# MLP token blocks of 384 and 512 columns, and weight tiles walked there and back

## The chip, the cores and the metric

The kernel runs on one core of a Trainium2 chip. The metric is the device time of that core in microseconds. TensorE does the matmuls, VectorE (DVE), ScalarE (ACT) and GpSimd (POOL) the work between them, and SyncE (SP) issues the DMAs.

## The reference

```python
def _attn_ref(q, k, v):                      # (4, 12, 448, 64) each
    scores = scale * np.matmul(q, k.transpose(0, 1, 3, 2))
    scores = np.where(mask, -1000000000.0, scores)      # causal
...
    return np.matmul(attn, v).astype(np.float32)
def _moe_ref(x, w1, w2, w3, w_out):          # x (1792, 768), d_ff 1024
    a = x @ w1
    b = x @ w2
    h = a * b @ w3
    return (h @ w_out).astype(np.float32)
def _moe2_ref(x, w_in, w_out):               # d_ff 2048
    h = x @ w_in
    g = h - np.tanh(h)
    return (g @ w_out).astype(np.float32)
def reference(**kwargs):
...
    x = np.ascontiguousarray(attn_out.transpose(0, 2, 1, 3)).reshape(B * S, H * D)
    x = _moe_ref(x=x, **moe_kwargs)
    return _moe2_ref(x=x, **moe2_kwargs)
```

## The kernel before

Activations lie transposed: features on the partitions, tokens along the columns. The 1792 tokens are taken in two halves of W = 896 columns, and each half of the MLPs in two blocks of S = 448 columns, one batch each. Every MLP operand is kept as a high and a low part (fp32r, `[P, 2, ...]`), and a product of one weight tile of 128 x 128 with one block is three matmuls in a row into one PSUM buffer, high by low, low by high, high by high (lines 406 to 408, in `gemms`). A product over 6, 8 or 4 such tiles is thus 18, 24 or 12 matmuls; each matmul has a weight load of its own.

The stages of a half, in order:
- `bilinear`: for each of 8 groups of 128 columns of W1 and W2, a weight tile `hl` of W1 (s = 0) and then one of W2 (s = 1), each with both blocks, 18 matmuls a block. Behind a product of W1, `keep` copies it to `asb`; behind one of W2, `mult` multiplies by `asb` (line 788), and `split` writes the high part (line 262) and the low part (line 265) of the result into the tile `g`.
- `project`: 6 weight tiles of W3·W_out, each with both blocks, 24 matmuls a block, reading `g`, writing `x` (the second half's is `x2`). That product of weights is made at the start of the kernel, beside attention, by matmuls of 384 columns (`product`).
- `Second.up`: 16 weight tiles of w_in, in four quarters q of 4, 18 matmuls a block. `finish` computes h - tanh(h) from the PSUM buffer, with tanh for large h and a polynomial for small, in some 12 instructions on ACT and DVE and a `split` into `g`, whose low part GpSimd writes.
- `Second.down`: for each quarter 6 weight tiles `w` of w_out, 12 matmuls a block, added up in `acc`; in the last quarter each block goes out by DMA (line 915).

The up products of a quarter and the down products of the quarter before are mixed by `paced`. While the second half goes through `bilinear` and `project`, the weights w_in and w_out are converted from float64 on DVE, ACT and POOL (tiles `raw`, `t`, `cvo`).

The order of the instructions on every engine comes from a planner (`Plan`): each strand of work is a generator that asks for a tile of a ring, an event or an engine with an assumed cost, such as `act(n)`, `dve(n)` or `pe(n, 3)`, and at each step the strand that could start first goes next. A ring hands out its buffers in turn. PSUM holds two buffers `mm`, to which six more, `mm2`, come once attention is over; these serve `project` of the second half and all that follows (`rings`).

Of the kernel before, what the change touches and what calls it, by code (L numbers as in the profile page):

```python
# [19 lines left out]
F32 = mybir.dt.float32  # L20
# [7 lines left out]
P = 128  # L28
# [3 lines left out]
NP = H // 2  # L32
W = 2 * S
OFF = [0, 112, 336, 672, 1120]

# [195 lines left out]
def body(ctx: ExitStack, tc: tile.TileContext, qkd, vd, vd4, w12, w3t, wo, w_in, wo2, out):  # L231
# [161 lines left out]
    def gemms(ring, n, products):  # L393
# [5 lines left out]
        for k in range(last + 1):  # L399
            for buf, (w, x, needs, finish) in zip(bufs, products):  # L400
# [366 lines left out]

    def bilinear(tiles, batches, x, xr, r_asb, ab, ab_ready):

        for j in range(8):  # L770
            asb, have = [None, None], [Event(), Event()]
            for s in range(2):
                wt = tiles[2 * j + s]
                yield wt.ready
                for t in batches:
                    tk = slice(t * S, (t + 1) * S)

                    def keep(buf, t=t, asb=asb, have=have):
                        asb[t] = yield r_asb
                        copy((yield [act(S, True), dve(S)]), asb[t].t[:, :S], buf.t[:, :S])  # L780
                        plan.done(buf)
                        plan.set(have[t])

                    def mult(buf, t=t, asb=asb, have=have, j=j, tk=tk):
                        yield have[t]
                        yield dve(S)
                        a = asb[t].t[:, :S]
                        V.tensor_tensor(out=a, in0=buf.t[:, :S], in1=a, op=ALU.mult)  # L788
                        plan.done(buf)
                        o = ab[j // 4].t  # L790
                        yield from split(S, o[:, 0, j % 4, tk], o[:, 1, j % 4, tk], a)
                        plan.done(asb[t])
                        plan.set(ab_ready[t][j])

                    def w(k, wt=wt):
                        return cols(wt.buf.t, k)

                    def xk(k, tk=tk):
                        return x[:, 0, k, tk], x[:, 1, k, tk]
                    yield from gemm(r_mm, S, w, xk, [[xr[t][k]] for k in range(NP)], (keep, mult)[s])  # L800
                plan.done(wt.buf)

    def project(tiles, ab, ab_ready, y, y_ready, rings):

        for m in range(6):
            wt = tiles[m]
            yield wt.ready
            for t in range(2):
                tk = slice(t * S, (t + 1) * S)

                def finish(buf, t=t, tk=tk, m=m):
                    hi, lo = y[:, 0, m, tk], y[:, 1, m, tk]
                    yield act(S, True)
                    A.copy(out=hi, in_=buf.t[:, :S])
                    yield dve(S)
                    sub("DVE", lo, buf.t[:, :S], hi.bitcast(F32))
# [9 lines left out]
                yield from gemm(next(rings), S, w, xk, [[ab_ready[t][k]] for k in range(8)], finish)  # L826
            plan.done(wt.buf)
        for a in ab:
            plan.done(a)


    class Second:
# [6 lines left out]

        def up(self, q, i):  # L840

            if i == 0:
                self.g[q] = yield r_g
                self.g_ready[q] = grid(2, 4)
            mm, t = divmod(i, 2)
            m = 4 * q + mm
            tk = slice(t * S, (t + 1) * S)
            wt = self.w_up[m]
            r = self.gp

            def finish(buf):
                h = buf.t[:, :S]
                sq, g = (yield r["sq"]), (yield r["g"])
                yield act(S, True)
                A.activation(out=sq.t, in_=h, func=AF.Square)  # L855
                th = yield r["th"]
                yield act(S, True)
                A.activation(out=th.t, in_=h, func=AF.Tanh)  # L858
                yield dve(S)
                V.scalar_tensor_tensor(out=g.t, in0=sq.t, scalar=LEAD, in1=h, op0=ALU.mult, op1=ALU.mult)  # L860
                yield dve(S)
                V.tensor_tensor(out=th.t, in0=h, in1=th.t, op=ALU.subtract)
                plan.done(buf)
                for k in range(3):
                    rk = yield r["r"]
                    yield act(S + 130)
                    A.activation(out=rk.t, in_=sq.t, func=AF.Square, bias=cst[:, k:k + 1])  # L867
                    if k == 2:
                        mk = yield r["r"]
                        if (yield [act(S + 130), dve2(S)]) == "ACT":  # L870
                            A.activation(out=mk.t, in_=sq.t, func=AF.Relu, bias=cst[:, 3:4])
                        else:
                            V.tensor_scalar(out=mk.t, in0=sq.t, scalar1=1.0, scalar2=None, op0=ALU.is_gt)
                        plan.done(sq)
                    yield dves(S)
                    V.scalar_tensor_tensor(out=g.t, in0=rk.t, scalar=QUAD[k][1], in1=g.t, op0=ALU.add, op1=ALU.mult)  # L876
                    plan.done(rk)
                yield dves(S)
                V.copy_predicated(out=g.t, mask=mk.t.bitcast(U32), data=th.t)
                plan.done(mk)  # L880
                plan.done(th)
                o = self.g[q].t
                yield from split(S, o[:, 0, mm, tk], o[:, 1, mm, tk], g.t)
                plan.done(g)
# [8 lines left out]
            yield from gemm(next(self.rings), S, w, xk, [[self.y_ready[t][k]] for k in range(NP)], finish,  # L893
                            [wt.buf] if t == 1 else [])

        def down(self, q, i):

            if self.acc is None:
                self.acc = yield self.acc_ring
            m, t = divmod(i, 2)  # L900
            tk = slice(t * S, (t + 1) * S)
            wt = self.w_down[6 * q + m]

            def finish(buf):
                a = self.acc.t[:, m, tk]
                if q == 0:
                    copy((yield [act(S, True), dve(S)]), a, buf.t[:, :S])
                else:
                    yield dve(S)
                    V.tensor_tensor(out=a, in0=buf.t[:, :S], in1=a, op=ALU.add)  # L910
                plan.done(buf)
                if q == 3:
                    yield dma(P * S * 4)
                    o = self.half * W + t * S
                    SP.dma_start(out=out[m, :, o:o + S], in_=a)
                    self.left -= 1
# [10 lines left out]
            yield from gemm(next(self.rings), S, w, xk, [[self.g_ready[q][t][k]] for k in range(4)], finish,  # L927
                            ([wt.buf] if t == 1 else []) + ([self.g[q]] if i == 11 else []))

# [24 lines left out]
    def first_half(cv, r_raw, r_t, x):  # L954
# [3 lines left out]
        for _ in range(2):  # L958
            ab.append((yield r_g))
        yield from bilinear(jobs_12, (0, 1), x.t, x_ready[:2], r_asb, ab, ab_ready[0])  # L960
        plan.done(x)
# [28 lines left out]
    with tc.tile_pool(name="late", bufs=1) as late, tc.tile_pool(name="mm2", bufs=1, space=PSUM) as mm2:  # L990
# [15 lines left out]
        def second_half(cv):  # L1006
            x = yield r_x2
            plan.spawn(fetch_x(x.t), -1)
            r_asb = Ring(cv, [P, S], F32, "asb", 4)
# [4 lines left out]
            yield from bilinear(w12s, (0, 1), x.t, x_ready[2:], r_asb, ab, ab_ready[1])  # L1014
            plan.done(x)
# [10 lines left out]
        with tc.tile_pool(name="gp", bufs=1) as gp:  # L1026
            rg = {k: Ring(gp, [P, S], F32, k, n) for k, n in (("sq", 2), ("th", 2), ("g", 3), ("r", 3))}
            r_acc = Ring(gp, [P, NP, W], F32, "acc", 1)
# [3 lines left out]
            def last():  # L1032
# [59 lines left out]
```

## Time and profile before

| | us |
|---|---|
| three timed runs | 1081.27, 1087.62, 1089.7 |
| their median | 1087.62 |
| the profiled execution | 1082.89 |
| its span, first to last instruction | 1081.1 |
| TensorE with a matmul in flight | 1054.2 |

The profile is one execution. Attention and the making of the weight products fill its first part, with the first half's `bilinear` from 183 to 366 us beside attention; then `project` to 424, the second half's `bilinear` to 542 and `project` to 600, and up and down products to 1077. Matmul records overlap, since a matmul's record runs to its last output, while the next one has begun: how fast TensorE goes is read from starts, not from the lengths of records.

### The profile page before, as it was taken

The page shows a single profiled execution, that of the slowest core. Times are in us where ns is not written, and L with a number is a line of the kernel's source. Part 1 is how long each engine was busy: PE and PEld are TensorE (multiplying, and loading weights), DVE is VectorE, ACT ScalarE, POOL GpSimd, SP SyncE. Part 2 cuts the span into 40 slices and gives each one's busy share as a digit, 9 for nine tenths or more (in the row PEclk, how much of TensorE's full clock was granted, in tenths as well). Part 3 has the DMA queues.
Part 4 walks back from the last instruction along what each step waited for, and adds up shares of the span by engine and source line. Part 5 has one row for each costly group of instructions (what it writes and reads, how often), then busy time and mean ns, then how long its engine had stood idle before and what let it go on. Part 6 is the DMA issues. An engine that isn't in the chain of part 4 may idle for free.

```text
span 1081.1 us, 19824 instructions
## 1 busy us (share of the span) xinstructions
PE 1054.2 (98%) x7680; PEld 927.5 (86%) x7680; DVE 643.9 (60%) x1319; ACT 617.3 (57%) x1354; POOL 230.0 (21%) x184
## 2 busy tenths in 40 slices
PE   6799999999999999999999999999999999999998
PEld 3577788788888999899999998999999999999997
DVE  7875556577563266565556576474756655374742
ACT  6998868787784244343333578563636456553620
POOL 3532132122223100123432222121111111110210
PEclk8999999999999999999999999999999999999999
DMA  7674359787652699999999632323333543233124
GB/s 260 208 215 162 112 169 305 254 284 250 235 190 107 221 340 313 314 337 336 323 346 321 257 117 88 117 98 107 108 109 113 176 142 99 93 113 117 40 90 149
DMA packets 72317, 209.03 MB, mean 193 GB/s; under 512 B 6112, under 2 KB 23008, under 8 KB 70688
## 3 DMA queue, kind: packets, MB, share of 16 engines
q1 hardware_dynamic: 72224, 207.77, 56.8%
q8 instruction: 60, 0.98, 0.4%
q14 instruction: 33, 0.27, 0.1%
HBM read 155.45 MB, written 52.30 MB: 192 GB/s over the span
## 4 chain that ended last, share of the span: by engine, by line
PE 79%; DMA 7%; DVE 7%; ACT 4%; issue 2%; POOL 1%; SPq 0%; DVEq 0%; ACTq 0%; POOLq 0%
PE mm L406 24%; PE mm L408 23%; PE mm L407 23%; DMA raw<-wo 4%; PE pv L671 3%; PE sc L645 2%; DVE t L312 1%; DVE p L447 1%; DVE t L309 1%; DVE t L316 1%; DMA raw<-w_in 1%; PE att L529 1%; DMA sco<-cvo 1%; PE att L476 1%; ACT p L489 1%
## 5 line engine op out<-in xcount | busy, mean ns | idle before, releaser
L406 PE MATMUL mm<-x,hl 128*128 128x448 f32 x768 | 286.4, 373 | 0.4 <-DVE asb L788 0.4
L407 PE MATMUL mm<-x,hl 128*128 128x448 f32 x768 | 282.0, 367 | 0.0
L408 PE MATMUL mm<-x,hl 128*128 128x448 f32 x768 | 282.0, 367 | 0.0
L406 PEld LDWEIGHTS mm<-x,hl 128*128 128x128 f32 x768 | 144.6, 188 | 17.9 <-issue 2.3
L408 PEld LDWEIGHTS mm<-x,hl 128*128 128x128 f32 x768 | 144.6, 188 | 13.1
L407 PEld LDWEIGHTS mm<-x,hl 128*128 128x128 f32 x768 | 144.7, 188 | 12.2
L265 POOL TENSOR_TENSOR g<-g 128x448 fp32r<-128x448 f32 x64 | 75.1, 1174 | 363.0 <-ACT g L262 363.0
L876 DVE SCALAR_TENSOR_TENSOR g<-r,g 128x448 f32<-128x448 f32 x192 | 124.4, 660 | 32.8 <-ACT r L867 29.5
L406 PE MATMUL mm<-g,w 128*128 128x448 f32 x384 | 141.4, 368 | 1.2 <-POOL g L265 1.2
L408 PE MATMUL mm<-g,w 128*128 128x448 f32 x384 | 141.3, 368 | 0.0
L407 PE MATMUL mm<-g,w 128*128 128x448 f32 x384 | 141.3, 368 | 0.0
L867 ACT ACTIVATE r<-sq,cst 128x448 f32<-128x448 f32 x192 | 121.8, 665 | 8.5 <-DVE g L876 8.4
L406 PE MATMUL mm<-g,hl 128*128 128x448 f32 (+1 forms) x320 | 116.9, 365 | 2.0 <-POOL g L265 2.0
L408 PE MATMUL mm<-g,hl 128*128 128x448 f32 (+1 forms) x320 | 113.5, 355 | 0.0
L407 PE MATMUL mm<-g,hl 128*128 128x448 f32 (+1 forms) x320 | 113.4, 354 | 0.0
L860 DVE SCALAR_TENSOR_TENSOR g<-sq,mm 128x448 f32<-128x448 f32 x64 | 39.7, 621 | 102.1 <-ACT th L858 102.1
L299 ACT ACTIVATE raw<-raw 128x512 uint32<-128x512 uint32 (+1 forms) x80 | 64.0, 800 | 54.3 <-DMA raw<-wo 23.6
L309 DVE TENSOR_SCALAR t<-raw 128x512 uint32<-128x512 uint32 (+1 forms) x80 | 51.6, 645 | 71.1 <-DMA raw<-wo 34.2
L855 ACT ACTIVATE sq<-mm 128x448 f32<-128x448 f32 x64 | 34.8, 543 | 102.8 <-PE mm L408 95.4
L265 POOL TENSOR_TENSOR hl<-t,hl 128x512 fp32r<-128x512 f32 (+1 forms) x32 | 52.2, 1636 | 147.6 <-ACT hl L262 112.5
L910 DVE TENSOR_TENSOR acc<-mm,acc 128x448 f32<-128x448 f32 x72 | 44.8, 622 | 62.5 <-PE mm L408 62.5
L406 PEld LDWEIGHTS mm<-g,w 128*128 128x128 f32 x384 | 72.1, 188 | 8.9 <-POOL g L265 1.6
(78 smaller groups left out, 1616.5 us busy)
## 6 DMA issues: line engine op xcount, KB each, us to landing
hl<-sci SPq DMA_DIRECT2D x32, 768.0 KB, 4.7
w<-sco SPq DMA_DIRECT2D x48, 512.0 KB, 3.5
raw<-w SPq DMA_DIRECT2D x16, 768.0 KB, 6.3
sc<-hl SPq DMA_DIRECT2D x16, 768.0 KB, 5.8
hl<-scp SPq DMA_DIRECT2D x12, 1024.0 KB, 7.3
raw<-w_in SPq DMA_DIRECT2D x16, 768.0 KB, 7.4
sci<-cvo SPq DMA_DIRECT2D x16, 768.0 KB, 6.9
hl<-sc SPq DMA_DIRECT2D x16, 768.0 KB, 5.8
```

The costliest lines, as they stand in the source:

```text
L265: (V if eng == "DVE" else G).tensor_tensor(out=out, in0=in0, in1=in1, op=ALU.subtract)
L299: A.activation(out=u, in_=u, func=AF.Copy, scale=2.0 ** -29)
L309: V.tensor_scalar(out=t, in0=raw[:, :n, 1], scalar1=3, scalar2=0x3FFFFFF8, op0=ALU.logical_shift_left, op1=ALU.bitwise_and)
L406: PE.matmul(ps, wh, xl, start=k == 0, stop=False)
L407: PE.matmul(ps, wl, xh, start=False, stop=False)
L408: PE.matmul(ps, wh, xh, start=False, stop=k == last)
L671: PE.matmul(ps.t[e * D:(e + 1) * D, a, have[0] * 32:P], v.t[r, kb, e], x, start=kb == 0, stop=kb == block(a, 4 - 1))
L855: A.activation(out=sq.t, in_=h, func=AF.Square)
L860: V.scalar_tensor_tensor(out=g.t, in0=sq.t, scalar=LEAD, in1=h, op0=ALU.mult, op1=ALU.mult)
L867: A.activation(out=rk.t, in_=sq.t, func=AF.Square, bias=cst[:, k:k + 1])
L876: V.scalar_tensor_tensor(out=g.t, in0=rk.t, scalar=QUAD[k][1], in1=g.t, op0=ALU.add, op1=ALU.mult)
L910: V.tensor_tensor(out=a, in0=buf.t[:, :S], in1=a, op=ALU.add)
```

## The change

The two blocks of a half become columns 0 to 383 and 384 to 895 (`BLOCKS`). The second reads tokens of both batches, so it waits for the inputs of both. Every size in `bilinear`, `project`, `up` and `down` follows the block, and the rings `asb`, `sq`, `th`, `g` and `r` of these stages get tiles of 512 columns. `there_and_back` gives the order of the blocks: 0, 1 for one weight tile, 1, 0 for the next, through all stages. `up` and `down` come to `paced` by weight tiles (4 and 6 a quarter, two blocks each) and no longer by blocks (8 and 12).

```diff
+BLOCKS = [(0, 384, (0,)), (384, 512, (0, 1))]
+BIG = 512
...
+    turn_at = [0]
+
+    def there_and_back():
+
+        turn_at[0] ^= 1
+        return (0, 1) if turn_at[0] else (1, 0)
+
...
                 wt = tiles[2 * j + s]
                 yield wt.ready
-                for t in batches:
-                    tk = slice(t * S, (t + 1) * S)
-
-                    def keep(buf, t=t, asb=asb, have=have):
+                for t in there_and_back():
+                    o, n, batches = BLOCKS[t]
+                    tk = slice(o, o + n)
+
+                    def keep(buf, t=t, n=n, asb=asb, have=have):
                         asb[t] = yield r_asb
-                        copy((yield [act(S, True), dve(S)]), asb[t].t[:, :S], buf.t[:, :S])
+                        copy((yield [act(n, True), dve(n)]), asb[t].t[:, :n], buf.t[:, :n])
...
-                    yield from gemm(r_mm, S, w, xk, [[xr[t][k]] for k in range(NP)], (keep, mult)[s])
+                    yield from gemm(r_mm, n, w, xk, [[xr[b][k] for b in batches] for k in range(NP)], (keep, mult)[s])
...
-            for t in range(2):
-                tk = slice(t * S, (t + 1) * S)
-
-                def finish(buf, t=t, tk=tk, m=m):
+            for t in there_and_back():
+                o, n, _ = BLOCKS[t]
+                tk = slice(o, o + n)
+
+                def finish(buf, t=t, n=n, tk=tk, m=m):
...
-        def up(self, q, i):
-
-            if i == 0:
+        def tile(self, kind, q, i):
+
+            for n, t in enumerate(there_and_back()):
+                yield from (self.up, self.down)[kind](q, i, t, n == 1)
+
+        def up(self, q, mm, t, last):
+
+            if q not in self.g:
...
-                        parts[0] += ([lambda z=z, q=q, i=i: z.up(q, i) for i in range(8)])
+                        parts[0] += ([lambda z=z, q=q, i=i: z.tile(0, q, i) for i in range(4)])
...
-                        parts[1] += ([lambda z=z, q=q, i=i: z.down(q, i) for i in range(12)])
+                        parts[1] += ([lambda z=z, q=q, i=i: z.tile(1, q, i) for i in range(6)])
```

Two places show what the change moves. The first is TensorE at the first weight tile of w_out, whose products read the first quarter's g (`g_6545`; `mm`, `mm2` and a number are PSUM buffers, `hl` and `w` weights; lines 406 to 408 have become 409 to 411). Before, the end of the tile's second product:

```order
L408 MATMUL mm2_6989<-g_6545,w_6546 128x448
L406 MATMUL mm2_6989<-g_6545,w_6546 128x448 [waits Pool_49]
L407 MATMUL mm2_6989<-g_6545,w_6546 128x448 [waits Activation_49]
L408 MATMUL mm2_6989<-g_6545,w_6546 128x448
L406 MATMUL mm2_7013<-x_4669,hl_6821 128x448 [waits DMAHW7_49,DVE_49]
```

Now, the end of its first product and the start of its second:

```order
L411 MATMUL mm_6975<-g_6545,w_6546 128x384
L409 MATMUL mm_6975<-g_6545,w_6546 128x384 [waits Pool_49]
L410 MATMUL mm_6975<-g_6545,w_6546 128x384 [waits Activation_49]
L411 MATMUL mm_6975<-g_6545,w_6546 128x384
L409 MATMUL mm2_6999<-g_6545,w_6546 128x512 [waits DVE_49]
```

The wait for the last tile of g of the quarter (its low part from GpSimd, its high part from ScalarE) stood at the fourth step of the second product; it stands now at the fourth step of the first, and the second waits for none.

The second place is VectorE at the end of the second half's `bilinear` and the start of its `project` (`asb_..<-mm_..` are the two `mult`, rows of `t` conversions, `x2_6058<-mm_6059` the first block of `project`; line 788 has become 799, 265 has become 268). Before:

```order
L788 TENSOR_TENSOR asb_5969<-mm_6001,asb_5969 128x448
L316 ISA t_5993<-raw_5962,t_5993 128x1024
L788 TENSOR_TENSOR asb_6002<-mm_6027,asb_6002 128x448
L309 TENSOR_SCALAR t_6045<-raw_5992 128x512
L312 SCALAR_TENSOR_TENSOR t_6045<-raw_5992,t_6045 128x512
L316 ISA t_6045<-raw_5992,t_6045 128x1024
L265 TENSOR_TENSOR x2_6058<-mm_6059,x2_6058 128x448
```

Now:

```order
L799 TENSOR_TENSOR asb_6002<-mm_6001,asb_6002 128x512
L799 TENSOR_TENSOR asb_5969<-mm_6029,asb_5969 128x384
L312 TENSOR_SCALAR t_6041<-raw_5992 128x512
L315 SCALAR_TENSOR_TENSOR t_6041<-raw_5992,t_6041 128x512
L319 ISA t_6041<-raw_5992,t_6041 128x1024
L268 TENSOR_TENSOR x2_6058<-mm_6059,x2_6058 128x384
```

The last two `mult` were blocks 0 and 1, and the first block of `project` was 0; now they are blocks 1 and 0, with `project` still beginning with 0, and the step of a conversion that stood between the two stands ahead of them.

## Rows read from the trace of the kernel before

**Rows 1.** The page, engines: busy us, share of the span, instructions.

```profile
PE 1054.2 (98%) x7680; PEld 927.5 (86%) x7680; DVE 643.9 (60%) x1319; ACT 617.3 (57%) x1354; POOL 230.0 (21%) x184
```

**Rows 2.** Groups by form on TensorE: count, then busy us and mean ns of one.

```profile
L407 PE MATMUL mm<-x,hl 128*128 128x448 f32 x768 | 282.0, 367 | 0.0
...
L407 PE MATMUL mm<-g,w 128*128 128x448 f32 x384 | 141.3, 368 | 0.0
...
L407 PE MATMUL mm<-g,hl 128*128 128x448 f32 x192 | 70.1, 365 | 0.0
```

**Rows 3.** Timeline of TensorE: start us, length us; 384 columns, then 448.

```profile
154.59 0.33 PE L407 MATMUL mm<-g,hl 128*128 128x384 f32 x1
...
158.75 0.33 PE L407 MATMUL mm<-g,hl 128*128 128x384 f32 x1
...
304.68 0.37 PE L407 MATMUL mm<-x,hl 128*128 128x448 f32 x1
...
307.99 0.37 PE L408 MATMUL mm<-x,hl 128*128 128x448 f32 x1
...
498.32 0.36 PE L406 MATMUL mm<-x,hl 128*128 128x448 f32 x1
...
527.51 0.36 PE L406 MATMUL mm<-x,hl 128*128 128x448 f32 x1
...
1032.73 0.37 PE L406 MATMUL mm<-g,w 128*128 128x448 f32 x1
...
1074.89 0.37 PE L406 MATMUL mm<-g,w 128*128 128x448 f32 x1
```

**Rows 4.** Stretches: TensorE busy us, granted clock, DMA share, GB/s.

```profile
152.00:158.90 6.90, 6.90 (x41) 1.00 0.49 159
305.00:308.00 3.00, 3.00 (x17) 1.00 0.99 344
498.00:527.00 29.00, 29.00 (x145) 1.00 0.92 304
1033.00:1075.00 42.00, 42.00 (x205) 1.00 0.41 130
```

**Rows 5.** Timeline at the first down products, TensorE and then GpSimd.

```profile
644.41 0.36 PE L406 MATMUL mm<-g,w 128*128 128x448 f32 x1
...
648.48 0.37 PE L408 MATMUL mm<-g,w 128*128 128x448 f32 x1
650.09 0.47 PE L406 MATMUL mm<-g,w 128*128 128x448 f32 x1 [1.25 <-POOL g L265]
...
648.91 1.13 POOL L265 TENSOR_TENSOR g<-g 128x448 fp32r<-128x448 f32 x1 [2.82 <-ACT g L262]
```

**Rows 6.** Waits of TensorE from 420 us to the end: us, times, longest.

```profile
PE mm L406 <- POOL g L265: 1.2, 1, 1.2
PE mm L406 <- DVE asb L788: 0.4, 2, 0.3
```

**Rows 7.** Groups by form, 650 us to the end.

```profile
L407 PE MATMUL mm<-g,w 128*128 128x448 f32 x377 | 138.7, 368 | 0.0
...
L407 PE MATMUL mm<-x,hl 128*128 128x448 f32 x312 | 114.8, 368 | 0.0
...
L910 DVE TENSOR_TENSOR acc<-mm,acc 128x448 f32<-128x448 f32 x72 | 44.8, 622 | 62.5 <-PE mm L408 62.5
```

**Rows 8.** Timeline at the two other handovers: TensorE, GpSimd, VectorE.

```profile
542.27 0.36 PE L406 MATMUL mm<-g,hl 128*128 128x448 f32 x1
...
600.63 0.36 PE L406 MATMUL mm<-x,hl 128*128 128x448 f32 x1
...
546.03 1.34 POOL L265 TENSOR_TENSOR g<-asb,g 128x448 fp32r<-128x448 f32 x1
...
603.13 0.62 DVE L265 TENSOR_TENSOR x<-mm,x 128x448 fp32r<-128x448 f32 x1
```

More of the change, by code (lines that the diff above doesn't have):

```diff
@@ L765, in product, with bilinear @@
             plan.done(t)
-    def bilinear(tiles, batches, x, xr, r_asb, ab, ab_ready):
+    def bilinear(tiles, x, xr, r_asb, ab, ab_ready):
         for j in range(8):
@@ L825, in xk @@
                     return a[:, 0, k % 4, tk], a[:, 1, k % 4, tk]
-                yield from gemm(next(rings), S, w, xk, [[ab_ready[t][k]] for k in range(8)], finish)
+                yield from gemm(next(rings), n, w, xk, [[ab_ready[t][k]] for k in range(8)], finish)
             plan.done(wt.buf)
@@ L851, in finish @@
             def finish(buf):
[L852 to L862, printed above, removed]
+                h = buf.t[:, :n]
+                sqb, gb = (yield r["sq"]), (yield r["g"])
+                sq, g = sqb.t[:, :n], gb.t[:, :n]
+                yield act(n, True)
+                A.activation(out=sq, in_=h, func=AF.Square)
+                thb = yield r["th"]
+                th = thb.t[:, :n]
+                yield act(n, True)
+                A.activation(out=th, in_=h, func=AF.Tanh)
+                yield dve(n)
+                V.scalar_tensor_tensor(out=g, in0=sq, scalar=LEAD, in1=h, op0=ALU.mult, op1=ALU.mult)
+                yield dve(n)
+                V.tensor_tensor(out=th, in0=h, in1=th, op=ALU.subtract)
                 plan.done(buf)
@@ L892, in up, with down @@
             yield wt.ready
-            yield from gemm(next(self.rings), S, w, xk, [[self.y_ready[t][k]] for k in range(NP)], finish,
-                            [wt.buf] if t == 1 else [])
-        def down(self, q, i):
+            yield from gemm(next(self.rings), n, w, xk, [[self.y_ready[t][k]] for k in range(NP)], finish,
+                            [wt.buf] if last else [])
+        def down(self, q, m, t, last):
             if self.acc is None:
                 self.acc = yield self.acc_ring
-            m, t = divmod(i, 2)
-            tk = slice(t * S, (t + 1) * S)
+            o, n, _ = BLOCKS[t]
+            tk = slice(o, o + n)
             wt = self.w_down[6 * q + m]
@@ L906, in finish @@
                 if q == 0:
-                    copy((yield [act(S, True), dve(S)]), a, buf.t[:, :S])
+                    copy((yield [act(n, True), dve(n)]), a, buf.t[:, :n])
                 else:
-                    yield dve(S)
-                    V.tensor_tensor(out=a, in0=buf.t[:, :S], in1=a, op=ALU.add)
+                    yield dve(n)
+                    V.tensor_tensor(out=a, in0=buf.t[:, :n], in1=a, op=ALU.add)
                 plan.done(buf)
                 if q == 3:
-                    yield dma(P * S * 4)
-                    o = self.half * W + t * S
-                    SP.dma_start(out=out[m, :, o:o + S], in_=a)
+                    yield dma(P * n * 4)
+                    d = self.half * W + o
+                    SP.dma_start(out=out[m, :, d:d + n], in_=a)
                     self.left -= 1
@@ L926, in down @@
             yield wt.ready
-            yield from gemm(next(self.rings), S, w, xk, [[self.g_ready[q][t][k]] for k in range(4)], finish,
-                            ([wt.buf] if t == 1 else []) + ([self.g[q]] if i == 11 else []))
+            yield from gemm(next(self.rings), n, w, xk, [[self.g_ready[q][t][k]] for k in range(4)], finish,
+                            ([wt.buf] if last else []) + ([self.g[q]] if last and m == 5 else []))
     def turns(*rings):
@@ L959, in first_half @@
             ab.append((yield r_g))
-        yield from bilinear(jobs_12, (0, 1), x.t, x_ready[:2], r_asb, ab, ab_ready[0])
+        yield from bilinear(jobs_12, x.t, x_ready[:2], r_asb, ab, ab_ready[0])
         plan.done(x)
@@ L1008, in second_half @@
             plan.spawn(fetch_x(x.t), -1)
-            r_asb = Ring(cv, [P, S], F32, "asb", 4)
+            r_asb = Ring(cv, [P, BIG], F32, "asb", 4)
             ab = []
@@ L1013, in second_half @@
                 ab.append((yield r_g))
-            yield from bilinear(w12s, (0, 1), x.t, x_ready[2:], r_asb, ab, ab_ready[1])
+            yield from bilinear(w12s, x.t, x_ready[2:], r_asb, ab, ab_ready[1])
             plan.done(x)
```

50 lines of the change are left out of this document (25 added, 25 removed).

## The prediction

> **What bounds the kernel now.** I read the shares of the engines first [rows 1]: TensorE has matmuls in flight for 98% of the span, VectorE and ScalarE are at 60% and 57%. That busy share doesn't say how fast TensorE goes: one matmul of 448 columns is recorded with 367 ns [rows 2], yet the next one starts after some 200 ns, so records overlap. What sets the time is the distance from start to start, and I read it next, from runs without a wait [rows 3]; the granted clock is 1.00 in all of these stretches [rows 4], so it isn't the clock.
> - 384 columns (the product W3·W_out): 24 distances from 154.59 to 158.75 us, 4.16/24 = 173.3 ns. At 2.4 GHz 384 columns are 160.0 ns: 13.3 ns are added.
> - 448 columns, bilinear stage of the second half: 144 distances from 498.32 to 527.51, 29.19/144 = 202.7 ns, 16.0 more than 186.7.
> - 448 columns, last stage: 204 distances from 1032.73 to 1074.89, 42.16/204 = 206.7 ns, 20.0 more.
> - The same 206.7 also stands early, 16 distances from 304.68 to 307.99 (3.31/16).
> So one shape has two rates, and the slow one isn't tied to a stage. The change of rate nearest to the end is the only long wait of the later stages: at 650.09 TensorE had stood for g [rows 5], the rate before it is 202.7, behind it 206.7 to the end. The three timed runs lie 8.4 us apart, and 4 ns on the 1965 early matmuls (counted below) would be 7.9 us, so I read the slower runs as ones with 206.7 early too. That is an estimate.
> Waits are small: behind 420 us the waits of TensorE for other engines are 1.2 us for g and 0.4 us for asb [rows 6].
>
> **The change, part by part.** *Counts.* As many matmuls, weight loads and other instructions as before, over as many columns: each pair 448 + 448 becomes 384 + 512, and only the added time of a matmul can differ. The MLPs have 768 + 384 + 192 groups of three in the rows of 448 columns [rows 2], 4032 matmuls; 377 + 312 of these groups start behind 650 us [rows 7], so 2067 are late (206.7) and 1965 early (202.7; some 50 us of that are mixed with attention and of both rates).
>
> *The price of 512.* No matmul of 512 columns stands in the trace. Low end: 213.3 ns and the 13.3 ns of the 384 row, 226.6. High end: the step from 384 to 448 late (206.7 - 173.3 = 33.4) taken once more, 240.1. Between lies one price for a column, 173.3/384, which gives 231.1 and would give 202.2 at 448, near the early rate. I take 226.6: the time added to 384 columns is the least of all, so the smallest claim on a fixed cost, and 448 columns add 13.3 and then 2.7 or 6.7 ns more, one or the other from wait to wait. I read this as a fixed 13.3 ns with something on top that comes and goes after a wait and that the 384 row doesn't show; that 512 don't show it either is a choice, and both ends stay in the range.
> - 226.6: mean of a pair (173.3 + 226.6)/2 = 200.0. Early 2.7 x 1965 = 5.3 us, late 6.7 x 2067 = 13.8 us: 19.1 us less.
> - 231.1: mean 202.2, 0.5 x 1965 + 4.5 x 2067 = 10.3 us less.
> - 240.1: mean 206.7, 4.0 x 1965 = 7.9 us more, late nothing.
>
> *The order within a pair.* A weight tile now ends with the block with which the next one begins, so three handovers get tighter; each is costed here [rows 5, 8].
> (a) First down products. Before, the last g of a quarter was wanted by the second product; now block 0 is finished last and wanted first, at the fourth step. The product began at 644.41 [rows 5]; nine matmuls of 173.3 later it is 645.97, and g was done at 648.91 + 1.13 = 650.04. TensorE would stand some 4 us, against 1.6 - 0.2 = 1.4 now (648.48 to 650.09): 2.6 us more, with nothing behind it but the last stage itself. In later quarters I count nothing: between a quarter's last up and its first down stand six products of the quarter before, 6 x 12 x 206.7 ns = 14.9 us.
> (b) Bilinear to project in the second half. The last product ended at 542.27, its low part was done by GpSimd at 546.03 + 1.34 = 547.37, 5.1 us behind, since conversions stand between on all three engines. The next product now wants it after 21 matmuls, 21 x 173.3 = 3.6 us: 1.5 us of waiting. Before, one more block lay between, and nothing waited. In the first half there are no conversions left and I count nothing.
> (c) Project to up: the low part ended at 603.13 + 0.62 = 603.75, 3.1 us behind 600.63; wanted after 15 x 173.3 = 2.6 us: 0.5 us.
> Two accumulators (mm) serve both bilinear stages, and the evacuation must now fit beside a block of 384 (18 x 173.3 = 3.1 us) instead of 448 (3.6 us) twice in four; it waited for 0.4 us [rows 6], and I add 0.5. The last block has 384 columns instead of 448, so the add behind the last matmul (622 ns at 448 [rows 7]) and its transfer are shorter: by a seventh of the add, 0.1 us, and as much for the transfer, 0.2 us less. Sum of the order: 2.6 + 1.5 + 0.5 + 0.5 - 0.2 = 4.9 us, taken as 5; from 0 (all three engines finish earlier than in the trace) to 9 (twice).
> The elementwise work keeps its instructions; an instruction's fixed part is paid as often, and VectorE and ScalarE stand idle for about 40%. Rings of 512 columns take more SBUF and no time. Ups now come two in a row and then two downs; eight accumulators hold them.
>
> *Sum.* The profiled run took 1082.89 us, 4.7 less than the median of 1087.62 and inside their spread (1081.27 to 1089.7). 1082.9 - 19.1 + 5 = 1068.8, taken as **1069 us**. A run of before that is slow early would gain 7.9 us more, so the gain over the median is larger than over the profiled run; the time after should be the same.
>
> **The rivals.** *The added time belongs to the stretch, not to the size.* Then 384 late would cost 160 + 20 = 180.0 and 512 213.3 + 20 = 233.3, a pair 413.3, as now; only the order is left: 1082.9 + 5 = 1088 us. For it: 448 has two rates at one size, and no 384 row stands behind 183 us. Against: over the 24 distances 384 columns keep to 173.3, and 448 change their rate inside one stretch, at a wait, with the same operands before and behind it.
> The Trainium skill (TensorE: Matmul & The Clock Gate, "Back-to-back issue gap") gives N/2.4 + 2.5 ns for a lone stream on a warm array, a fixed cost whatever the size. By it, too, the split of 896 columns would change nothing, but the added time here, 13.3, 16.0 and 20.0 ns [rows 3], is neither 2.5 nor fixed.
>
> *One price per column* (231.1): 1082.9 - 10.3 + 5 = 1077.6 us, about 0.9% under the median. For it: it fits 384 exactly and 448 early within 0.5 ns. Against: the late rate, which no price per column gives, and that 448 hold two of them.
>
> *512 columns pay more than 384 save.* The added time grows with the columns, 13.3, 20.0 and then 26.8 ns, in every block 1 of the MLPs: 1082.9 + 7.9 + 5 = 1095.8 us, slower than the median by 0.8%. It decides from the mean at which the gain is used up: the matmuls now average (1965 x 202.7 + 2067 x 206.7)/4032 = 204.75 ns, the 5 us are 1.2 ns each, so a pair's mean of 203.5, so a block of 512 at 233.7 ns. Against: the early rows lie on a flatter line, 13.3 and 16.0, which would go on to 18.7.
>
> **How the numbers follow.** Chances: fixed 13.3 ns, 1069 us: 0.47; one price per column, 1078: 0.20; the stretch, 1088: 0.18; growing, 1096: 0.10; other 0.05. The first case alone spans 1063 (order costs nothing) to 1073. The range goes to 1089 to take in the next two; 0.15 lies above, little below 1062. A measurement of this kernel can tell about 1% from no change, that is 1076.7 and 1098.5 around the median. Faster: 0.47 and half of the second case, 0.57. Slower: a part of the growing case with a larger order cost, and of the rest, 0.07. Within 1%: 0.36.
>
> **What the profile after would show.** Distances of 173.3 ns in blocks of 384 in every stage, and of 226.6 in blocks of 512, with no second rate: that is the step on which all rests, and 231 or more at 512, or 180 at 384 late, gives it to a rival. A wait of some 4 us for g at the first down product, one of 1 to 2 us for GpSimd's or ScalarE's g at the start of the second project, one below 1 us at the first up; more than 9 us of waits behind 420 us would show the order mis-sized. A product with the first rate early and the second late would show that what I read as the property of a size is one of a state.

## The result, and the profile after

The changed kernel takes 1071.39 us (median of 6 runs, 1070.05 to 1075.8), the kernel before, timed beside it, 1086.89 us (6 runs, 1078.85 to 1090.27). The ratio is 0.9882, with a 95% interval from 0.9837 to 0.9928: 1.2% faster. Ratios, here and below, are the recorded ones, taken from the runs that lie within 1.5% of the fastest of their kernel, and can differ by some 0.0025 from the quotient of the medians beside them. The profiled run of the changed kernel took 1072.49 us with a span of 1070.7 us; that of before took 1082.89 us.

The engines on the page of the changed kernel (busy us, share of the span, instructions), to lay beside [rows 1]:

```profile
PE 1043.1 (97%) x7680; PEld 903.0 (84%) x7680; DVE 636.3 (59%) x1319; ACT 619.8 (58%) x1353; POOL 233.6 (22%) x185
```

The number of matmuls is the same and TensorE is as full as before; the matmuls have become cheaper. What one costs is again read from start to start. TensorE in the second half's project stage of the changed kernel, from the timeline (start us, length us), answers to [rows 3]:

```profile
559.79 0.33 PE L409 MATMUL mm<-g,hl 128*128 128x384 f32 x1
...
563.95 0.33 PE L409 MATMUL mm<-g,hl 128*128 128x384 f32 x1
...
564.47 0.39 PE L409 MATMUL mm<-g,hl 128*128 128x512 f32 x1
...
566.55 0.39 PE L409 MATMUL mm<-g,hl 128*128 128x512 f32 x1
...
569.27 0.39 PE L409 MATMUL mm<-g,hl 128*128 128x512 f32 x1
...
574.71 0.39 PE L409 MATMUL mm<-g,hl 128*128 128x512 f32 x1
575.39 0.33 PE L409 MATMUL mm<-g,hl 128*128 128x384 f32 x1
...
576.46 0.33 PE L409 MATMUL mm<-g,hl 128*128 128x384 f32 x1
```

From 559.79 to 563.95 lie 24 distances of 384 columns: 4.16/24 = 173.3 ns. From 569.27 to 574.71 lie 24 of 512: 5.44/24 = 226.7 ns. Both are 13.3 ns over the columns at 2.4 GHz. Where the size changes, a little is added for a few matmuls: the first nine distances at 512 (564.47 to 566.55) take 2.08 us where nine of 226.7 ns are 2.04, and the first six at 384 (575.39 to 576.46) take 1.07 us where six of 173.3 ns are 1.04. That is some 41 and 26 ns, 33 ns for a change of size in the mean.

The stretches of the changed kernel (us, TensorE's busy us, granted clock, DMA share, GB/s), which answer to [rows 4], the last two rows at the start of the program and at the first down products:

```profile
559.00:576.00 17.00, 17.00 (x85) 1.00 0.88 313
652.00:1060.00 408.00, 408.00 (x2032) 1.00 0.35 114
0.00:60.00 60.00, 41.82 (x239) 0.89 0.65 218
648.00:651.00 3.00, 3.00 (x9) 0.50 0.00 0
```

The granted clock is 1.00 throughout the MLPs but for the row at 648 us. Why it is 0.50 there shows in the timeline of TensorE and, below it, GpSimd, which answers to [rows 5]:

```profile
643.63 0.34 PE L411 MATMUL mm<-g,w 128*128 128x384 f32 x1
646.87 0.44 PE L409 MATMUL mm<-g,w 128*128 128x384 f32 x1 [2.90 <-POOL g L268]
...
647.50 0.51 PE L409 MATMUL mm<-g,w 128*128 128x512 f32 x1
...
651.15 0.39 PE L409 MATMUL mm<-g,w 128*128 128x512 f32 x1
...
645.82 0.99 POOL L268 TENSOR_TENSOR g<-g 128x384 fp32r<-128x384 f32 x1 [2.23 <-ACT g L265]
```

Nine matmuls into the first down product, TensorE waits for the quarter's last g, which GpSimd ends at 645.82 + 0.99 = 646.81 us. From 643.63 to 646.87 are 3.24 us, 3.07 more than a distance of 173.3 ns. Behind it the clock stays at half for a while: nine distances of 512 columns, 647.50 to 651.15, take 3.65 us instead of 2.04, 1.6 us more. TensorE's waits from 360 us to the end of the changed kernel (us, times, longest) answer to [rows 6]:

```profile
PE mm L409 <- POOL g L268: 3.3, 2, 2.9
PE mm L409 <- DVE asb L799: 0.5, 1, 0.5
```

By stages, each from its first matmul to the next stage's first in the two timelines (ups: the first 12, downs: from the first down to the last matmul, with the later ups):

```
us                     before    after   difference
start to bilinear      183.15   186.25   +3.10
bilinear, half 1       182.86   179.38   -3.48
project, half 1         58.36    57.92   -0.44
bilinear, half 2       117.89   116.84   -1.05
project, half 2         58.37    58.45   +0.08
first 12 ups            43.78    43.40   -0.38
downs                  432.75   424.69   -8.06
behind last matmul       3.95     3.78   -0.17
span                  1081.11  1070.71  -10.40
```

### The profile page after: what moved, and what is told of

Its sections match the earlier page's. It is cut to its first block, busy times and chain, and to the rows that moved or that the text cites. A ratio compares the mean times of both kernels' runs of the same rounds, so it can differ in the third digit from the quotient of the medians.

```text
span 1070.7 us, 19817 instructions
## 1 busy us (share of the span) xinstructions
PE 1043.1 (97%) x7680; PEld 903.0 (84%) x7680; DVE 636.3 (59%) x1319; ACT 619.8 (58%) x1353; POOL 233.6 (22%) x185
## 4 chain that ended last, share of the span: by engine, by line
PE 78%; DMA 9%; DVE 5%; ACT 4%; issue 2%; POOL 1%; SPq 0%; DVEq 0%; ACTq 0%; POOLq 0%
PE mm L409 23%; PE mm L410 22%; PE mm L411 22%; DMA raw<-wo 3%; PE pv L681 3%; DMA raw<-w_in 2%; PE sc L655 2%; PE att L539 2%; DMA sco<-cvo 2%; PE att L486 2%; PE att L511 1%; DVE t L315 1%; DVE t L319 1%; DVE t L312 1%; ACT p L499 1%
## 5 line engine op out<-in xcount | busy, mean ns | idle before, releaser
L409 PE MATMUL mm<-x,hl 128*128 128x384 f32 (+1 forms) x768 | 282.2, 367 | 0.5 <-DVE asb L799 0.5
L411 PE MATMUL mm<-x,hl 128*128 128x384 f32 (+1 forms) x768 | 278.9, 363 | 0.0
L410 PE MATMUL mm<-x,hl 128*128 128x384 f32 (+1 forms) x768 | 278.7, 363 | 0.0
L268 POOL TENSOR_TENSOR g<-g 128x384 fp32r<-128x384 f32 (+1 forms) x64 | 76.9, 1201 | 353.4 <-ACT g L265 353.4
L409 PE MATMUL mm<-g,w 128*128 128x384 f32 (+1 forms) x384 | 139.8, 364 | 2.9 <-POOL g L268 2.9
L411 PE MATMUL mm<-g,w 128*128 128x384 f32 (+1 forms) x384 | 140.2, 365 | 0.0
L410 PE MATMUL mm<-g,w 128*128 128x384 f32 (+1 forms) x384 | 140.1, 365 | 0.0
L895 DVE SCALAR_TENSOR_TENSOR g<-r,g 128x512 f32<-128x512 f32 (+1 forms) x192 | 124.7, 659 | 21.3 <-ACT r L886 18.9
L886 ACT ACTIVATE r<-sq,cst 128x384 f32<-128x384 f32 (+1 forms) x192 | 123.6, 666 | 7.1 <-DVE g L895 7.1
L409 PE MATMUL mm<-g,hl 128*128 128x384 f32 (+1 forms) x320 | 116.7, 365 | 2.2 <-POOL g L268 2.2
L410 PE MATMUL mm<-g,hl 128*128 128x384 f32 (+1 forms) x320 | 112.8, 353 | 0.0
L411 PE MATMUL mm<-g,hl 128*128 128x384 f32 (+1 forms) x320 | 112.8, 353 | 0.0
L879 DVE SCALAR_TENSOR_TENSOR g<-sq,mm 128x384 f32<-128x384 f32 (+1 forms) x64 | 39.6, 620 | 111.5 <-ACT th L877 110.9
L312 DVE TENSOR_SCALAR t<-raw 128x512 uint32<-128x512 uint32 (+1 forms) x80 | 49.3, 616 | 68.9 <-DMA raw<-wo 29.9
L873 ACT ACTIVATE sq<-mm 128x384 f32<-128x384 f32 (+1 forms) x64 | 34.7, 542 | 94.2 <-PE mm L411 88.1
L319 DVE CUSTOM_DVE_ANT_0 t<-raw,t 128x1024 uint16<-128x1024 uint16 (+1 forms) x80 | 74.8, 935 | 8.2 <-ACT raw L302 1.5
```

The source lines that it names most:

```text
L268: (V if eng == "DVE" else G).tensor_tensor(out=out, in0=in0, in1=in1, op=ALU.subtract)
L312: V.tensor_scalar(out=t, in0=raw[:, :n, 1], scalar1=3, scalar2=0x3FFFFFF8, op0=ALU.logical_shift_left, op1=ALU.bitwise_and)
L319: V.tensor_tensor(out=t, in0=t, in1=raw[:, :n, 0], op=ALU.add)
L409: PE.matmul(ps, wh, xl, start=k == 0, stop=False)
L410: PE.matmul(ps, wl, xh, start=False, stop=False)
L411: PE.matmul(ps, wh, xh, start=False, stop=k == last)
```

## The experiments

Each is the changed kernel with the edit shown, unless said. Where no diff is shown the kernel is one already described. The kernel before was run beside each group of them: 1080.71 us (median of 19 runs, 1069.94 to 1088.11) beside the first four, 1078.32 (31 runs, 1072.06 to 1092.44) beside the next four, 1078.32 (23 runs, 1071.02 to 1085.87) beside the last three.

**The sizes without the order.** Every weight tile takes block 0 and then block 1.

```
     def there_and_back():
-        turn_at[0] ^= 1
-        return (0, 1) if turn_at[0] else (1, 0)
+        return 0, 1
```

> Blocks of 384 and 512 columns, but block 0 first for every weight tile. Theory (the sizes carry the gain): steady distances stay 173.3 and 226.7 ns; the size now changes twice a weight tile, 123 more changes at some 33 ns (the trace after shows about 40 ns behind a change to 512 and 26 behind one to 384) are 4.1 us more; the three handovers ease again, so the wait at the first down product falls from 3.1 us to 1.4 or less and the clock doesn't drop there, 3.4 us less, and the wait of 0.5 us at the second project goes: 1071.4 + 4.1 - 3.9 = 1071.6 us, 1.5% under before. Rival (the order carries the gain, since a weight tile that begins with the last block saves something on TensorE): most of the gain goes, 1082 us or more.

Measured: 1075.37 us (10 runs, 1073.14 to 1079.88), ratio 0.9951 (0.9922 to 0.998). The distances are again 173.3 and 226.7 ns. But two of its parts came out otherwise than I had thought. The size now changes twice for each weight tile, not once, and the mean distances in the last stage are 175.3 and 229.8 ns against 174.3 and 228.2 in the changed kernel. And the wait at the first downs did not ease. TensorE in this kernel, from the timeline, the granted clock behind the wait, and GpSimd:

```profile
646.43 0.39 PE L411 MATMUL mm<-g,w 128*128 128x512 f32 x1
649.68 0.79 PE L409 MATMUL mm<-g,w 128*128 128x512 f32 x1 [2.86 <-POOL g L268]
...
650.00:653.00 3.00, 3.00 (x9) 0.50 0.16 37
...
648.37 1.27 POOL L268 TENSOR_TENSOR g<-g 128x512 fp32r<-128x512 f32 x1 [4.44 <-ACT g L265]
```

The wait has moved to the second product, yet is about as long, 3.0 us: the first down begins at 642.24 us as in the changed kernel, but the last g is done at 649.64 and not at 646.81. From the first up to the last matmul this kernel takes 470.8 us and the changed kernel 468.1, both with a wait of some 3 us and the half clock behind it; the 80 changes of size more that lie there, at 33 ns each, make 2.6 of the 2.7 us. So the sizes alone make the kernel faster, and the order of the blocks adds to it by halving the changes of size. The second part is read from this stage of one trace each; the two kernels weren't run beside each other, and their ratios' intervals overlap.

**The order without the sizes.**

```
-BLOCKS = [(0, 384, (0,)), (384, 512, (0, 1))]
-BIG = 512
+BLOCKS = [(0, 448, (0,)), (448, 448, (1,))]
+BIG = 448
```

> Blocks of 448 columns as before, walked there and back, up and down paced by weight tile. Theory (sizes): distances of 202.7 and 206.7 ns as before, and the order's waits on top, some 4 us at the first down product (with a drop of the clock if the wait is as long as now) and below 1 us at the second project: 1087 + 3 to 5 = 1090 to 1092 us. Rival (order): faster than before by half of the gain or more, 1079 us or less.

Measured: 1082.66 us (10 runs, 1078.62 to 1088.44), ratio 1.003 (0.9995 to 1.0066): the order alone gives nothing. Its trace holds more than that. TensorE in this kernel, from the timeline, and GpSimd:

```profile
551.25 0.37 PE L411 MATMUL mm<-g,hl 128*128 128x448 f32 x1
552.24 0.47 PE L409 MATMUL mm<-g,hl 128*128 128x448 f32 x1 [0.62 <-POOL g L268]
552.55 0.37 PE L410 MATMUL mm<-g,hl 128*128 128x448 f32 x1
...
653.82 0.37 PE L411 MATMUL mm<-g,w 128*128 128x448 f32 x1
654.39 0.47 PE L409 MATMUL mm<-g,w 128*128 128x448 f32 x1 [0.21 <-POOL g L268]
654.70 0.36 PE L410 MATMUL mm<-g,w 128*128 128x448 f32 x1
...
1075.64 0.37 PE L411 MATMUL mm<-g,w 128*128 128x448 f32 x1
...
653.19 1.15 POOL L268 TENSOR_TENSOR g<-g 128x448 fp32r<-128x448 f32 x1 [2.83 <-ACT g L265]
```

From 552.55 to 653.82 lie 490 distances, 101.27/490 = 206.7 ns; from 654.70 to 1075.64 lie 2077, 420.94/2077 = 202.7 ns. The rate changes at the two waits and nowhere between. Here a wait ends the slow rate at the very place where, in the run of before [rows 5], a wait began it. Not every wait changes it: two earlier waits in this trace, 0.8 us at 516 and 0.9 us at 539, left 202.7 ns as it was.

The wait of some 4 us that I expected at the first down didn't come either. It is 0.4 us, from 653.82 to 654.39 less one distance: the first down begins at 652.17 us, and the last g is done at 654.34, 2.2 us behind, where it was 5.6 behind in the trace of before. From the first down on this kernel, with blocks of 448, takes 423.5 us, 1.2 less than the changed kernel with its long wait.

**Another block first at the first down.** One flip there, so that the block finished last isn't the one wanted first.

```
+            if kind == 1 and q == 0 and i == 0 and self.half == 0:
+                turn_at[0] ^= 1
```

> The new kernel with one more turn ahead of the first down tile, which so begins with block 1, whose g is done one block earlier. Theory (the wait of 3.1 us there and the 3.4 us at half clock behind it are paid in the end time): the first product waits for nothing, the second some 1.3 us, too short for the clock; 1071.4 - 3.5 = 1068 us. Rival (the elementwise chain is what is late, and the wait goes to the next product or the next up): 1071 us, the waits behind 640 us still 3 us or more in sum.

Measured: 1069.66 us (4 runs, 1067.37 to 1071.85), ratio 0.9899 (0.9856 to 0.9942). TensorE where the wait for g would be, from the timeline, and all its waits from 360 us on:

```profile
645.81 0.39 PE L409 MATMUL mm<-g,w 128*128 128x512 f32 x1
646.04 0.40 PE L410 MATMUL mm<-g,w 128*128 128x512 f32 x1
646.27 0.39 PE L411 MATMUL mm<-g,w 128*128 128x512 f32 x1
...
PE mm L409 <- POOL g L268: 1.3, 1, 1.3
```

The rows run on; the 1.3 us left are at the second project. Ups and downs together, from the first up to the last matmul, take 463.3 us, and 468.1 in the changed kernel: the wait of 3.07 us and the 1.6 of the half clock are gone. The 1.3 us expected at the second product didn't come. Turning the order at this one place thus takes the wait away; how long it is doesn't follow from the order, as the two kernels above show (0.4 us with the order alone, 3.0 with the sizes alone).

**The first down later.** The downs of a first quarter begin further behind its ups.

```
-    def paced(*parts):
+    def paced(*parts, lag=0.3):
-        todo = sorted((0.7 * (i + 0.5) / len(p) + 0.3 * n, n, i) ...
+        todo = sorted((0.7 * (i + 0.5) / len(p) + lag * n, n, i) ...
-                    yield from paced(*parts)
+                    yield from paced(*parts, lag=0.5 if k == 1 else 0.3)
```

> The new kernel with the first quarter's down products moved behind one more up tile (7.2 us). Theory: g is done some 1.6 us ahead of its first use, no wait and no drop of the clock at the first down: 1071.4 - 4.8 = 1066.6 us. Rival (three up tiles more in a row fill the accumulators, since the elementwise work of an up takes 4.7 us and its matmuls 3.6): a wait for an accumulator of 1 to 4 us comes in its place, 1068 to 1071 us.

Measured: 1067.77 us (4 runs, 1065.38 to 1070.53), ratio 0.989 (0.9841 to 0.9939). No wait of TensorE for another engine is left behind 360 us, and ups and downs, counted in the same way, again take 463.3 us against 468.1. The expectation counted up to another end, some 1 us further on, in both kernels; the difference is what it tells.

**The same in the kernel before.** The last edit, made in the kernel before (blocks of 448, the old order).

> The kernel before with the first quarter's down products moved behind two more up products (7.3 us), so that TensorE has no wait there. Theory (448 columns hold either rate, 202.7 or 206.7 ns, and change it only at a wait): no wait behind 650 us, so the last stage keeps the rate with which it begins, one rate from the first up to the end; with 202.7 the last stage is some 8 us shorter than in the trace before, and the wait of 1.4 us goes too. Rival (the rate belongs to the stage, its tiles or its eight accumulators): 206.7 ns from about 650 us on again, 1 to 2 us under before.

Measured: 1075.63 us (10 runs: eight from 1071.6 to 1077.1, two above 1087), ratio 0.9994 (0.995 to 1.0038); the profiled run took 1076.24. TensorE in it, from the timeline:

```profile
458.06 0.36 PE L407 MATMUL mm<-x,hl 128*128 128x448 f32 x1
...
603.77 0.36 PE L406 MATMUL mm<-x,hl 128*128 128x448 f32 x1
...
1070.51 0.37 PE L408 MATMUL mm<-g,w 128*128 128x448 f32 x1
```

There is no wait between, and one rate: 612.45/3022 = 202.7 ns to the end. The last stage isn't slow by itself: in the profiled run of before the rate changed at the wait at its head, and here, without that wait, it doesn't change.

From the first up (603.77) to the last matmul are 466.7 us, and 476.5 in the trace of before: the rate over the last stage and the wait. This is also the fair comparison for the sizes, since the later first down with blocks of 384 and 512 has no wait there either. Its first up and last matmul:

```profile
596.53 0.33 PE L409 MATMUL mm<-x,hl 128*128 128x384 f32 x1
...
1059.82 0.34 PE L411 MATMUL mm<-g,w 128*128 128x384 f32 x1
```

These are 463.3 us, 3.4 less; over 2303 distances that is 1.5 ns for each, and it is what the sizes save against 448 columns at their fast rate.

In the whole time this kernel shows no gain over before (0.9994), though its trace is 9.8 us shorter in that stage. That suggests that most runs of before beside it weren't slow to the end either; they have no traces that could show it. The two runs above 1087 us would fit the slow rate over many stages, but they have no trace either.

**Other sizes of the two blocks**, 416 + 480, 400 + 496, and (one run) 432 + 464:

```
-BLOCKS = [(0, 384, (0,)), (384, 512, (0, 1))]
-BIG = 512
+BLOCKS = [(0, 416, (0,)), (416, 480, (0, 1))]
+BIG = 480
```

> The new kernel with blocks of 416 and 480 columns, multiples of 32 and not of 128. Theory (a fixed 13.3 ns for any size, and a second rate only at 448): 186.7 and 213.3 ns, a mean of 200.0, the time of the new kernel, 1070 to 1072 us. Rival (multiples of 128 alone are free of what 448 pay on top): distances above these by 2.7 to 6.7 ns, as at 448, uneven or of two rates, 1074 to 1084 us.

> The new kernel with blocks of 400 and 496 columns, multiples of 16 only. Theory (fixed 13.3 ns): 180.0 and 220.0 ns, mean 200.0, 1070 to 1072 us. Rival (multiples of 128): each 2.7 to 6.7 ns more, 1074 to 1084 us.

> Blocks of 432 and 464 columns, for the distances alone. The runs so far add 13.4 ns at 384, 13.4 at 400, 14.7 at 416, 16.0 or 20.0 at 448, 17 to 20 at 480, 19.9 at 496 and 13.4 at 512. Theory (what is added rises from 400 to 512 and falls back at 512): 432 columns 15 to 17 ns above 180.0, 464 columns 16 to 20 above 193.3. Rival (only single sizes are bad, 448, 480 and 496): 13.3 at both, 193.3 and 206.7 ns.

Measured: 416 + 480 takes 1081.99 us (10 runs, 1077.37 to 1084.67), ratio 1.0027 (0.9994 to 1.0059); 400 + 496 takes 1081.19 (10 runs, 1077.15 to 1086.91), ratio 1.001 (0.997 to 1.005); 432 + 464 took 1083.15 in its one run. No gain in any, so a fixed 13.3 ns with a second rate only at 448 is out: it gave 1070 to 1072 us for the first two. Their time has another part, the waits at the first down, 4.3 and 2.4 us, with the clock at half behind both. TensorE in the kernel of 416 + 480, from the timeline, first and last start of four blocks:

```profile
449.49 0.35 PE L409 MATMUL mm<-x,hl 128*128 128x416 f32 x1
...
456.08 0.35 PE L411 MATMUL mm<-x,hl 128*128 128x416 f32 x1
...
464.11 0.35 PE L409 MATMUL mm<-x,hl 128*128 128x416 f32 x1
...
470.64 0.35 PE L411 MATMUL mm<-x,hl 128*128 128x416 f32 x1
470.83 0.37 PE L409 MATMUL mm<-x,hl 128*128 128x480 f32 x1
...
478.29 0.38 PE L411 MATMUL mm<-x,hl 128*128 128x480 f32 x1
...
485.29 0.38 PE L409 MATMUL mm<-x,hl 128*128 128x480 f32 x1
...
492.99 0.38 PE L411 MATMUL mm<-x,hl 128*128 128x480 f32 x1
```

A block has 35 distances: 416 columns take 6.59/35 = 188.3 ns in one and 6.53/35 = 186.6 in another, 480 columns 7.46/35 = 213.1 and 7.70/35 = 220.0 (a block's reading is good to 0.3 ns). The rate changes from block to block, with no wait between these blocks, only a change of size. Then 496 columns, in the kernel of 400 + 496:

```profile
426.72 0.38 PE L409 MATMUL mm<-x,hl 128*128 128x496 f32 x1
...
434.64 0.39 PE L411 MATMUL mm<-x,hl 128*128 128x496 f32 x1
```

7.92/35 = 226.3 ns: 16 columns fewer than 512 save nothing. With the other readings, taken in the same way over several blocks (what is added to the columns at 2.4 GHz, ns):

```
columns   384    400    416         432    448         464    480                496    512
added     13.3   13.4   13.3/15.1   15.9   16.0/20.0   19.8   13.3/17.7/20.0     19.9   13.3
```

The least, 13.3, stands in every block that was read at 384 and 512 columns, and within 0.1 ns at 400. So it isn't multiples of 128 alone that are cheap, but none of the six sizes tried between 400 and 512 keeps to 13.3. 400 + 496 cost (180.1 + 226.5)/2 = 203.3 ns in the mean, no better than 448 at its fast rate, and 384 + 512 cost 200.0.

**The changed kernel again**, once among the four kernels of the second group, and once beside the kernel with the later first down.

> The new kernel once more, beside the others on the same chip. Theory: no second rate, so its runs lie close together, 1070 to 1073 us, whatever before does there, while the runs of before spread over 10 us and more. Rival (the spread is the chip's, not the rate's): it spreads as before does.

> The new kernel with the first quarter's down products behind one more up tile, again, with more rounds and beside the new kernel. Theory (the wait and the half clock behind it are the only cost of the new order that is left): 4.5 us less than the new kernel in the same call. Rival (the three us of the first comparison were the spread): within 1.5 us of it.

> The new kernel in the same call: 1070 to 1073 us, 3 to 5 us above the one with the later first down.

Measured: the changed kernel 1070.57 us (10 runs, 1067.67 to 1077.34), ratio 0.9921 (0.9891 to 0.9951), and 1072.74 (12 runs, 1067.44 to 1076.96), ratio 0.994 (0.9913 to 0.9968); the later first down 1070.78 (12 runs, 1065.7 to 1073.96), ratio 0.9918 (0.9888 to 0.9948). In the profiled runs the first-down wait stands again in the changed kernel (3.2 and 2.8 us idle, with ups and downs of 468.0 both times), and ups and downs again take 463.3 us in the other. Yet the medians of the runs that stood side by side differ by 2.0 us, between the 4.5 expected and the 1.5 of the rival and within the spread of either: the 4.8 us are plain in the stage and not resolved in the whole time. Nor do the runs of the changed kernel lie as close together as expected: 9.7 and 9.5 us from the lowest to the highest, where those of before beside them span 20.4 and 14.9 us. Part of the spread is thus not the second rate's. One source of it is in the trace of the later first down, in its waits of TensorE, a stretch of its second project, and ScalarE:

```profile
PE mm L409 <- POOL g L268: 2.3, 1, 2.3
...
548.00:551.00 3.00, 2.85 (x8) 0.54 0.80 291
...
544.99 0.62 ACT L265 CAST cvo<-t 128x512 fp32r<-128x512 f32 x1 [2.93 <-DMA sco<-cvo]
545.52 0.51 ACT L265 CAST g<-asb 128x384 fp32r<-128x384 f32 x1
```

The same kernel had no wait at that place in its first trace. The last g of the stage stands on ScalarE behind a conversion of weights, and that conversion waited 2.93 us for a DMA that carries an earlier converted tile away; in the first trace it waited 1.18 us for the same.

## Why the prediction was right, step by step

**The price of 512 columns, on which all rested, was right.** 226.7 ns were measured and 226.6 taken; 384 columns cost 173.3 in the late stages as in the early one. No block of 384 or 512 that was read in any of the traces had a second rate. That removes three rivals: the added time that belongs to the stretch (384 late would be 180.0), one price per column (512 would be 231.1) and the one that grows (512 would be 233 or more). The last has something to it all the same: what is added does grow from 400 to 496 columns in most blocks, and then falls back at 512. The choice of the low end was right, and the reason that I gave for it, a fixed 13.3 ns with something on top, describes the table above without explaining it; with this reason alone 416 + 480 and 400 + 496 were expected to do as well, and they didn't.

**The late rate was sized too large, by a term I didn't have.** I took 6.7 ns for each late matmul, 13.8 us. The downs have 2088 matmuls; without waits and half clock they took (424.69 - 4.7)/2087 = 201.2 ns each, not 200.0, against (432.75 - 1.4)/2087 = 206.7 before: 11.4 us. The missing 2.4 us are the changes of size: each weight tile has one, 33 ns in the mean, and 74 of the 124 tiles lie in this stage (48 of the downs and, with 936 of the matmuls at 36 for a tile, 26 of the ups), 74 x 0.033 = 2.4 us. Taking the two blocks of every tile in the same order makes them twice as many, as the kernel with the sizes alone showed.

**The wait at the first down** was foreseen at its place and about its size, 3.07 us for "some 4", but its size is in part luck. I took the last g to be ready as in the trace of before, 5.6 us behind the start of the first down product. It was ready 4.6 us behind it here (646.81 - 642.24), 2.2 us with the order alone and 7.4 us with the sizes alone. When the elementwise work ends thus moves from kernel to kernel by more than the whole wait. Not foreseen was the half clock behind it, 1.6 us. Together 4.7 against 1.4 before is 3.3 us more, where 2.6 stood in the sum. The two kernels that take the wait away, by another block order or a later start, show it by removing both. The Trainium skill (TensorE: Matmul & The Clock Gate, "HAM oscillation — how this bites in real kernels") has TensorE restart at the lower clock when its waits between bursts of matmuls are long enough; the trace agrees, with 0.50, the lower of its two levels, behind the wait of 3.07 us. Behind the 1.4 us of before [rows 5] it stayed at 1.00, as this stretch of the kernel before shows (columns as in [rows 4]):

```profile
652.00:655.00 3.00, 3.00 (x17) 1.00 0.45 167
```

The 2.3 us in the trace of the later first down were enough for 0.54.

**The smaller handovers cost less than I took.** The second project waited 0.5 us in the profiled run (taken: 1.5), the first up not at all (0.5), and asb held TensorE 0.5 us against 0.4 before (0.5 more). The tail gave back 0.17 us (0.2). The first of them isn't a constant: it was nothing in one trace of the later first down and 2.3 us in another.

**The early matmuls.** Predicted were 5.3 us from the rate less 2.5 of waits, 2.8 us; the early stages gave back 5.27 us (the five rows of the table from the first bilinear to the ups). The waits were some 1.9 us smaller, as said. The 50 tiles of these stages have a change of size each, some 1.7 us at 33 ns that I hadn't counted. And 3.48 us come from the first bilinear stage, of which some 1.5 aren't the change's at all: in the trace of before the clock fell to half there, as these rows show (the stretch with columns as in [rows 4], then the timeline).

```profile
199.00:202.00 3.00, 3.00 (x11) 0.51 0.57 162
...
199.24 0.74 PE L406 MATMUL mm<-x,hl 128*128 128x448 f32 x1
...
202.39 0.40 PE L408 MATMUL mm<-x,hl 128*128 128x448 f32 x1
```

The eight distances from 199.24 to 202.39 take 3.15 us instead of some 1.63. The first trace of the changed kernel has 1.00 over the same stretch, but a later trace of it has such a drop at 204 us, so the drop belongs to the run. What is left, 2.8 + 1.9 - 1.7 + 1.5 = 4.5 against 5.27, is 0.8 us that I can't lay to one cause: 480 matmuls of that stage lie among those of attention, nearly 100 us and not the 50 that I took, and have either rate there.

**The sum** was near for reasons that offset each other. The profiled run gave 1082.89 - 10.40 = 1072.49 us for the 1068.8 worked out: 2.5 us better early, 3.1 worse late, and 3.1 lost before the first bilinear product. The order of the instructions up to there is the same; the granted clock of the first 60 us was 0.89, and 0.94 in before. Both values also stand in two traces of one kernel, the later first down (0.94 and 0.89), so this belongs to a run and not to the change. Taken together, the time up to the end of the first bilinear stage is nearly the same in both traces, 366.01 and 365.63 us: the 3.1 lost and the 3.48 gained all but cancel, and the gain of this pair of runs lies behind it.

**The base was misread in one thing.** I took the slow rate behind 650 us as what before costs there, and only the early part as varying. The runs show that the late rate varies too: a kernel with blocks of 448 has it at 202.7 ns to the end when the last wait leaves it so, and at 206.7 when not. Against the first, the change saves 1.5 ns a matmul; against the second, 5.5 ns. So of the 11.4 us that the late matmuls gave back in this pair of traces, some 8.3 (4.0 ns x 2087) are owed to the rate that before had in its trace, and 3.1 would be left against the other. Over all the matmuls of the MLPs the ends are 4032 x 1.5 = 6 us and 4032 x 5.5 = 22 us, less the new wait. It fits, without proving it, that the runs of before spread over some 20 us (1069.94 to 1092.44 in all) and that the ratio moved between groups of runs, 0.988, 0.992 and 0.994, while the medians of the changed kernel stayed at 1070.6 to 1072.7. The gain holds in each of the three intervals; that it is over 1%, the forecast's likeliest, holds by the ratio of one of the three, and the interval of the last lies wholly under 1%.

**Open**: why 416, 448 and 480 columns have several rates and what in a wait picks one; why a change of size costs its 41 and 26 ns; and why the DMA that holds up the second project takes longer in some runs. Blocks under 384 columns weren't tried.

## What to carry to other kernels

Read a matmul's cost from start to start, stretch by stretch, and over several sizes: sizes of 384 and 512 columns had the least added time here, 496 cost as much as 512, and 448 had two prices. With blocks of unequal size, end one weight tile and begin the next with the same block, but look at each handover where the block that is finished last is now wanted first: a wait of 3 us cost another 1.6 in clock. Before a gain is worked out from one trace of before, look whether the same shape runs at another rate elsewhere in it; if so, the base itself has two values, and one trace shows one of them.

## What of the hardware I had not expected

Added time that isn't a function that rises with the size (13.3 ns at 384, 19.9 at 496, 13.3 at 512); a rate at one shape that can change at a wait and then holds for up to 3022 matmuls, 202.7 or 206.7 ns at 448 columns; and 33 ns in the mean for each change between blocks of 384 and 512 columns, spread over the next six to nine matmuls.
